# Attention output turned by DMA for 31 of 32 pairs of heads, in place of 16, and another written order of the attention's steps

## The chip, the cores and the metric

The kernel runs on one core of one Trainium2 chip. The metric is the device time of one execution in microseconds (us), lower is better. The engines are TensorE (PE in the profile; PEld is its weight load), VectorE (DVE), ScalarE (ACT), GpSimd (POOL) and SyncE (SP, which here only issues DMAs). Each engine runs its own instructions strictly in the order in which they were written into the program.

## The reference

Two stages, cut to what matters:

```python
def phi(x):
    proj = np.einsum('bhsd,df->bhsf', x, w_phi)
    proj = proj - np.max(np.abs(proj), axis=-1, keepdims=True)
    return np.concatenate([np.exp(proj), np.exp(-proj)], axis=-1)
q_p, k_p = phi(q), phi(k)                  # q, k, v: 8 batches, 8 heads, 576 tokens, 64
kv = einsum('bhsf,bhsd->bhfd', k_p, v);  z = k_p.sum(axis=2)
x = (q_p @ kv) / (q_p @ z + 1e-6)          # -> 4608 tokens x 512

P = exp(x @ w_gate - max)                  # 8 experts
for _ in range(8):                         # Sinkhorn routing
    P /= P.sum(1); P /= P.sum(0); P *= N / E
out = sum_e P[:, e] * (relu(x @ w1[e]) @ w2[e])     # w1: 512x1024, w2: 1024x512
```

## The kernel before

**Attention.** The unit of work is a pair of heads of one batch: 8 batches of 4 pairs, 32 in all. A pair's 576 tokens are 512 "main" tokens in four tiles of 128, and 64 "rest" tokens that all four pairs of a batch share as one extra tile. For a pair, TensorE projects k and q (L622), DVE takes the maxima (`maxes`, L614), ACT the exponentials (`exp`, L618), POOL scales v, TensorE forms kv and then the numerators with the denominator as a 65th column (L905), and DVE scales them, takes the reciprocal (L918) and writes the quotient to the tile `xb` (L919), tokens on the partitions.

**Turning.** The expert stage needs x with features on the partitions, in the resident tile `xT`. `pair_c` does this for the 512 main tokens of one pair, in one of two ways. On TensorE: four 128x128 transposes against an identity into a PSUM bank (L934), then one DVE copy of 128x512 to `xT` (L937). By DMA: one transposing DMA of 128 KB on SP's queue (L928), which reads `xb` and writes `xT`, with no PSUM bank and no DVE work. Before the change batches 3 to 6, 16 pairs, go by DMA and the rest by TensorE. The rest tokens of a batch always go by TensorE (`rest_c`, L944, copies L949). `gate` (16 tiny matmuls per 512 tokens) and expert 0's first product then read `xT`.

**Expert 0 as fill.** Expert 0 needs no routing weights, so its matmuls are put among the attention's: `up0` (8 matmuls of 512 columns over `xT` and w1, then ReLUs on ACT into `hx`, L983) and `down0` (8 matmuls of 512 columns over `hx` and w2). 24 such ups and 20 downs are written among the attention's steps; 12 ups and 16 downs more follow it and cover the routing, a chain of small DVE operations with one tiny matmul (L1179, output of `cs`) in each of 8 iterations. Then come experts 1 to 7 (L1466, L1475), the bulk of the time.

**What sets the order.** Each operation is recorded with a cost, its reads and writes, and its buffers. `Plan.schedule` then runs a model of the engines and of the two DMA queues: at each point the operation that can start first goes next, ties to the one recorded earlier, and the result is the written order of every engine. The string `order` sets in which order the attention's steps are recorded, one letter a step: `l` and `e` load q, k, v and the rest tokens; `w` loads a piece of expert 0's weights; `t` turns raw q and k by DMA (L567); `r` is the rest tokens' part; `a`, `q`, `p` are k's part, q's maxima and q's features of the next pair; `b` forms kv, `n` and `m` the outputs of the pair's two heads; `c` is `pair_c`; `g` is `rest_c` and `gate` of a batch; `u` and `d` are one `up0` and one `down0`.

SP's queue carries the loads of q and k for batches 0 and 1 (L544), of v (L558) and of rest tokens (L600, L607), the turning of raw q and k (L567, L686), and the turned outputs (L928). POOL's queue carries the casting loads of q and k for the other batches (L550, L605) and of expert 0's weights (L527, L531), between POOL's own arithmetic.

Of the kernel before, what the change touches and what calls it, by code (L numbers as in the profile page):

```python
# [349 lines left out]
def kernel(  # L350
# [13 lines left out]
    B, H, S, D = q.shape  # L364
# [4 lines left out]
    NP = H // 2  # L369
# [43 lines left out]
    def pe(cols, fn, r=(), w=(), takes=()):  # L413
        plan.op("PE", max(cols / 2400.0 + 0.0025, 0.031), 0.22, fn, r, w, takes)
# [4 lines left out]
    def dve(el, fn, r=(), w=(), shared=False):  # L419
        plan.op("DVE", el / 960.0 + 0.07, 0.15, fn, r, w, shared=shared)  # L420
# [7 lines left out]
    def dma(queue, nbytes, rate, fn, r=(), w=()):  # L428

        speed, unit = LINK.get(rate, (rate, 40))  # L430
        if nbytes == 2 << 20:
            speed, unit = 400, 150
        o = plan.op(queue, 0.8 if queue == "POOL" else 0.6, 0.0, fn, r, w, (), nbytes / speed)
        o.turn, o.unit = rate == 148, unit
# [71 lines left out]
    def new(tag):  # L506
        return R[tag].new()

    def bf(buf):

        return buf().bitcast(BF16)
# [412 lines left out]
        return xb, outs  # L924

    def pair_c(b, pr, xb):
        if b in (3, 4, 5, 6,):
            dma("SP", 1 << 17, 148, lambda: nc.sync.dma_start_transpose(  # L928
                out=xT[:, pr, b * SM:(b + 1) * SM].rearrange("p (a c) -> p a c", c=128),
                in_=xb()[:, 0:NJ].rearrange("p a b -> p (a b)")), [(xb, 0), (xb, 1)], [("xT", b, pr)])  # L930
            return
        pxt = new("PP")
        for j in range(NJ):
            pe(128, lambda j=j: nc.tensor.transpose(  # L934
                bf(pxt)[:, j * 128:j * 128 + 128], xb()[:, j, :], ident),
                [(xb, 0), (xb, 1), "ident"], [pxt])
        dve(270, lambda: nc.vector.tensor_copy(  # L937
            out=xT[:, pr, b * SM:(b + 1) * SM], in_=bf(pxt)[:, 0:512]),
            [pxt], [("xT", b, pr)])
# [150 lines left out]
    def stage_g(b):  # L1090
# [7 lines left out]
             "r": stage_r, "b": stage_b,  # L1098
             "n": lambda j: kvs[j](0), "m": lambda j: kvs[j](1),
             "c": lambda j: pair_c(j // 4, j % 4, xbs[j]), "g": stage_g,  # L1100
             "u": lambda i: up0(i // 4, i % 4), "d": lambda i: down0(i // 4, i % 4)}
    order = (
        "lraeaepqbwlqaqawwabwmqlltnrbppnwqbppmrmanbqaqmwwacmpnpbccpwbtcnmqnaqbclupunm"
        "taumquglcapalbcpnqqdcenmucugbblnapmrcqdutabnqpmunpbambccddnqplanmqmducpblttb"
        "augnaqlnrbdcampcadmqeutunqcppmdcaqtdqabpbbmlrqtdnpmuaqualbnagnacctbmqulupran"
        "tdpmtdqcmdnpdabdancpcabbqmpumqbcdgnappqunburqcbugmmnqdcdanumupqbnucmcpnmbddp"
        "bqmpncncubncmmgccg"
    )
    for i, n in enumerate(order):
        at[0] = i  # L1110
# [948 lines left out]
```

## Time and profile before

| | |
|---|---|
| median of 3 runs | 1009.96 us (1009.75 to 1012.1) |
| span of the profiled execution, first to last instruction | 1008.8 us |
| attention and its fill, by the last L905 and L937 | 0 to about 203 us |
| transposing DMAs of the output (L928) | 16 |
| TensorE transposes of the output (L934) and their DVE copies (L937) | 64 and 16 |
| granted TensorE clock | 1.000 |

The profile is one execution. Of the medians' 1009.96 us, 1008.8 us lie between its first and last instruction. Busy time of PE is modelled: matmuls are pipelined, each shown with its full latency, so the price of a matmul in a row of them is read from the distance between starts, not from its duration.

### The profile page before, as it was taken

What the parts mean: (1) busy time and instruction counts of PE and PEld (TensorE: products, weight loads), DVE (VectorE), ACT (ScalarE), POOL (GpSimd) and SP (SyncE); (2) the same over time, 40 slices, a digit from 0 to 9 for tenths busy, and PEclk for the clock granted to TensorE, in tenths of its full rate; (3) what the DMA queues carried; (4) which work ended last, traced back from release to release, by engine and by line L of the source; (5) the groups of instructions that cost most, each with busy time, mean ns of one, the idle gap of its engine ahead of it and who ended that gap; (6) DMA issues with size and microseconds to landing.
All of it is one profiled execution on the core that took longest, in us unless ns stands there. A gap on an engine that the chain in (4) does not pass through costs nothing.

```text
span 1008.8 us, 23309 instructions
## 1 busy us (share of the span) xinstructions
PE 994.0 (99%) x8376; PEld 727.7 (72%) x8376; DVE 898.6 (89%) x1999; ACT 812.8 (81%) x1930; POOL 447.6 (44%) x514
## 2 busy tenths in 40 slices
PE   7899999999999999999999999999999999999998
PEld 5666666644566877777777877787778777787775
DVE  7999998987888998899989898989889988989886
ACT  7999999845979788878878788777887888778874
POOL 5778674400133344434444444444443444344443
PEclk9999999999999999999999999999999999999999
DMA  9999999181136423282327133632246222724653
GB/s 249 183 202 183 157 153 144 38 170 56 53 121 143 147 97 98 84 184 96 109 98 170 44 100 131 130 127 98 97 117 177 97 98 84 147 79 142 208 174 126
DMA packets 129748, 128.86 MB, mean 128 GB/s; under 512 B 55776, under 2 KB 98272, under 8 KB 129632
## 3 DMA queue, kind: packets, MB, share of 16 engines
q1 hardware_dynamic: 97680, 103.33, 36.3%
q0 software_dynamic: 31648, 23.86, 16.9%
q8 instruction: 65, 1.06, 0.5%
q14 instruction: 51, 0.42, 0.2%
q10 hardware_dynamic: 304, 0.20, 0.1%
HBM read 122.50 MB, written 19.53 MB: 141 GB/s over the span
## 4 chain that ended last, share of the span: by engine, by line
PE 92%; DVE 3%; ACT 2%; DMA 2%; issue 1%; POOL 0%; DVEq 0%
PE ps L1466 41%; PE ps L1475 20%; PE ps L622 17%; PE ps L1607 11%; PE ps L905 2%; DMA xi6t<-X 1%; DMA xi<-X 1%; PE ps L752 1%; ACT q L618 0%; DVE m L614 0%; ACT k L618 0%; DVE wx L614 0%; DVE X L1240 0%; DMA acc<-in_k_dram 0%; DVE hs L1676 0%
## 5 line engine op out<-in xcount | busy, mean ns | idle before, releaser
L1875 POOL TENSOR_TENSOR acc<-acc,hx 128x512 f32<-128x512 f32 x186 | 236.1, 1276 | 404.7 <-ACT hx L1872 135.0
L1466 PEld LDWEIGHTS <-hs 128*128 128x128 bf16 x1984 | 194.1, 98 | 46.4 <-issue 0.2
L1872 ACT ACTIVATE hx<-ps,P 128x256 f32<-128x256 f32 x372 | 158.9, 483 | 53.4 <-PE ps L1466 52.0
L1860 DVE SCALAR_TENSOR_TENSOR acc<-ps,P,acc 128x256 f32<-128x256 f32 x372 | 162.2, 478 | 30.2 <-PE ps L1466 28.2
L1475 PE MATMUL ps<-xT,T 128*128 128x512 bf16 x608 | 171.0, 379 | 0.0
L1466 PEld LDWEIGHTS <-hx 128*128 128x128 bf16 x1488 | 145.6, 98 | 24.9
L1466 PE MATMUL ps<-hx,hs 128*128 128x256 bf16 x992 | 144.3, 273 | 0.0
L1676 DVE CUSTOM_DVE_ANT_0 hs<-ps,U 128x512 bf16<-128x512 f32 x192 | 124.7, 684 | 11.3 <-PE ps L1475 6.6
L1607 PE MATMUL ps<-xT 128*128 128x256 bf16 x576 | 125.4, 272 | 0.0
L1475 PEld LDWEIGHTS <-T 128*128 128x128 bf16 x672 | 65.8, 98 | 40.6
L1682 ACT ACTIVATE hs<-ps 128x512 bf16<-128x512 f32 x96 | 55.9, 598 | 41.7 <-PE ps L1475 40.2
L1466 PE MATMUL ps<-wx,hs 128*128 128x256 bf16 x560 | 78.4, 273 | 0.0
L622 PE MATMUL ps<-w,hx 128*128 128x512 bf16 x288 | 73.0, 379 | 0.0
L622 PE MATMUL ps<-xT,w 128*128 128x512 bf16 x288 | 72.9, 379 | 0.0
L1466 PE MATMUL ps<-wx,hx 128*128 128x256 bf16 x496 | 72.3, 273 | 0.0
L1676 DVE CUSTOM_DVE_ANT_0 hs<-ps,X 128x512 bf16<-128x512 f32 x96 | 65.1, 684 | 7.8 <-PE ps L1607 6.9
L1466 PE MATMUL ps<-hx 128*128 128x256 bf16 x496 | 71.2, 273 | 0.0
L1607 PEld LDWEIGHTS <-xT 128*128 128x128 bf16 x576 | 56.3, 98 | 17.5
L1466 PE MATMUL ps<-w,hx 128*128 128x256 bf16 x432 | 62.2, 273 | 0.0
L614 DVE TENSOR_REDUCE m<-ps 128x4 f32<-128x512 f32 x88 | 58.8, 680 | 3.7 <-PE ps L622 1.9
L1672 ACT COPY X<-ps 128x512 f32<-128x512 f32 x96 | 58.6, 610 | 2.5 <-DVE ps L1650 2.5
L1466 PE MATMUL ps<-w,hs 128*128 128x256 bf16 x432 | 60.2, 273 | 0.0
(174 smaller groups left out, 2256.0 us busy)
## 6 DMA issues: line engine op xcount, KB each, us to landing
xT<-xi SPq DMA_DIRECT2D x48, 448.0 KB, 4.6
xT<-xd SPq DMA_DIRECT2D x72, 256.0 KB, 4.0
wx<-in_moe_w_dram POOLq DMA_DIRECT2D x8, 1024.0 KB, 11.2
v_m<-in_v_dram SPq DMA_DIRECT2D x15, 512.0 KB, 5.2
out_dram<-acc SPq DMA_DIRECT2D x14, 512.0 KB, 3.0
w<-in_moe_w_dram POOLq DMA_DIRECT2D x6, 1024.0 KB, 11.0
xT<-xp SPq DMA_DIRECT2D x24, 256.0 KB, 2.8
qk<-in_k_dram POOLq DMA_DIRECT2D x12, 256.0 KB, 5.4
```

The source lines that it names most:

```text
L614: dve(el, lambda: nc.vector.tensor_reduce(out=dst(), in_=src(), axis=AX.X, op=ALU.max, apply_absolute_value=True), r, w)
L622: nc.tensor.matmul(out_, lhsT=lhsT, rhs=rhs, start=start, stop=stop)
L905: pe(65, lambda j=j: nc.tensor.matmul(pn()[:, j * D1:j * D1 + D1], lhsT=s["T"][x]()[:, j % 2, 2 * h + j // 2, :] if j < 4 else r["T"][x]() ...
L1466: pe(256, lambda i=i, k=k, z=z: nc.tensor.matmul(bank()[:, 256 * i:256 * i + 256], lhsT=lhs(k, i), rhs=rhs(k), start=first and z, stop=k = ...
L1475: pe(512, lambda k=k: nc.tensor.matmul(bank().rearrange("p (a b) -> p a b", a=2), lhsT=lhs(k), rhs=rhs(k), start=first and k == 0, stop=k ...
L1607: pe(256, lambda: nc.tensor.matmul(halves_of(bank[q], n)(), lhsT=lhs(), rhs=t()[:, rhs, :], start=start, stop=True, skip_group_check=True) ...
L1672: act(512, lambda: nc.scalar.copy(out=flat(to[q])(), in_=bank[q]()), [bank[q]], [(to[q], 0), (to[q], 1)])
L1676: dve(515, lambda: nc.vector._custom_dve(ADD_SAT, out=out_(q, i, j), in0=bank[q]().rearrange("p (a b) -> p a b", a=2), in1=to[q](), s0=3.0 ...
L1682: act(512, lambda: nc.scalar.activation(out=out_(q, i, j), in_=bank[q]().rearrange("p (a b) -> p a b", a=2), func=ACT.Relu, bias=0.0, scal ...
L1860: dve(320, lambda n=n, ts=ts: nc.vector.scalar_tensor_tensor(out=acc[g][:, ts, 256 * j:256 * j + 256], in0=bank()[:, 256 * n:256 * n + 256 ...
L1872: act(370, lambda n=n: nc.scalar.activation(out=u()[:, n, :], in_=bank()[:, 256 * n:256 * n + 256], func=ACT.Copy, bias=0.0, scale=P[:, 4 ...
L1875: pool(695, lambda: nc.gpsimd.tensor_tensor(out=acc[g][:, 2 * i:2 * i + 2, 256 * j:256 * j + 256], in0=acc[g][:, 2 * i:2 * i + 2, 256 * j: ...
```

## The change

`pair_c` sends every pair but the very last, (batch 7, pair 3), by DMA. That is 15 pairs more: batches 0, 1 and 2, and three pairs of batch 7. The string `order` is another one, with the same count of each letter.

```diff
     def pair_c(b, pr, xb):
-        if b in (3, 4, 5, 6,):
+        if (b, pr) != (B - 1, NP - 1):
             dma("SP", 1 << 17, 148, lambda: nc.sync.dma_start_transpose(
                 out=xT[:, pr, b * SM:(b + 1) * SM].rearrange("p (a c) -> p a c", c=128),
...
     order = (
-        "lraeaepqbwlqaqawwabwmqlltnrbppnwqbppmrmanbqaqmwwacmpnpbccpwbtcnmqnaqbclupunm"
...
+        "raqllbaapqenwalqabrpnmwwpwbmmnwwqqbpmbcwtpnecacapqqwacgllupbmpqlanqnubcnttbl"
...
```

Since the planner makes the order anew, rows move on every engine in the attention's part. From the expert stage on the orders agree: the last 70 per cent of the rows stand in the same order on PE, ACT, DVE and SP.

SP's queue early in the attention, before (`v_m` and `v_r` are v, `qk` and `qk_r` raw q and k, `qkT` and `rT` the same turned; a number behind x counts equal rows):

```order
L544 DMA acc_79<-in_q_dram 128x4x256
L607 DMA v_r<-in_v_dram 64x8x64 x2
L686 DMA_TRANSPOSE rT<-qk_r 128x4x128 x2
L558 DMA v_m<-in_v_dram 128x4x256
L567 DMA_TRANSPOSE qkT<-qk 128x16x128 x2
L558 DMA v_m<-in_v_dram 128x4x256 x2
L567 DMA_TRANSPOSE qkT<-qk 128x16x128
```

The same place of SP's queue now:

```order
L607 DMA v_r<-in_v_dram 64x4x64
L928 DMA_TRANSPOSE xT<-xb 128x4x128 x2
L558 DMA v_m<-in_v_dram 128x4x256
L607 DMA v_r<-in_v_dram 64x8x64 x2
L567 DMA_TRANSPOSE qkT<-qk 128x16x128
L928 DMA_TRANSPOSE xT<-xb 128x4x128 x2
L558 DMA v_m<-in_v_dram 128x4x256
L928 DMA_TRANSPOSE xT<-xb 128x4x128
L686 DMA_TRANSPOSE rT<-qk_r 128x4x128 x2
L928 DMA_TRANSPOSE xT<-wx 128x4x128
```

The outputs of batch 0 now stand in this queue, pairs 0 and 1 ahead of a load of v, pairs 2 and 3 behind the first turning of raw q and k; before, the queue held no L928 here.

DVE around the last outputs of batch 0, before (L937 is the copy of a turned pair; the last `xb` of batch 0 is the row `xb<-ps,wx`, whose reciprocal lies in the tile wx):

```order
L919 TENSOR_TENSOR xb<-ps,rec 128x5x64
L937 COPY xT<-ps 128x512
L913 TENSOR_TENSOR ps<-ps,r 128x325
L937 COPY xT<-ps 128x512 x2
L918 RECIPROCAL wx<-ps 128x5
L919 TENSOR_TENSOR xb<-ps,wx 128x5x64
L614 TENSOR_REDUCE m<-ps 128x4
L614 TENSOR_REDUCE m_r<-ps 128x2x2 x2
L892 COPY kv<-ps 128x260
L937 COPY xT<-ps 128x512
```

The same place on DVE now:

```order
L919 TENSOR_TENSOR xb<-ps,wx 128x5x64
L614 TENSOR_REDUCE wx<-ps 128x4
L614 TENSOR_REDUCE m<-ps 128x4
L614 TENSOR_REDUCE wx<-ps 128x4
L892 COPY kv<-ps 128x260
L614 TENSOR_REDUCE m<-ps 128x4
L614 TENSOR_REDUCE wx<-ps 128x4
L614 TENSOR_REDUCE m<-ps 128x4
L614 TENSOR_REDUCE wx<-ps 128x4
L614 TENSOR_REDUCE m<-ps 128x4
L949 COPY xT<-ps 64x4x64 x2
```

The four copies L937 of batch 0 are gone; behind the last `xb` stand eight maxima of later pairs, and then the copies of batch 0's rest tokens, which now come before the first fill instead of well after it.

More of the change, by code (lines that the diff above doesn't have):

```diff
@@ L1102 @@
     order = (
-        "lraeaepqbwlqaqawwabwmqlltnrbppnwqbppmrmanbqaqmwwacmpnpbccpwbtcnmqnaqbclupunm"
[L1104 to L1107, printed above, removed]
+        "raqllbaapqenwalqabrpnmwwpwbmmnwwqqbpmbcwtpnecacapqqwacgllupbmpqlanqnubcnttbl"
+        "munuaadrcptqmtcmculabmapabdqmrnaqpuneucbqdnmupaqacbdpmctlnbcdqumaplblntmgpuq"
+        "dabanlntpdqqacupqbrmguebccndnqmaaltbcpdalrumbqnpdqbcgmqpuubabcmnmpqundctqrcp"
+        "nbdagmpatuadnmubpmauaqnnbdpbncmuqdpqccncbmpmtccddgnpauqbprqbdpbanmmdmdnucnmu"
+        "cpqpbccqnumbgnmccg"
     )
```

## The prediction, on record before the changed kernel ran

> **What bounds the kernel now.** I read the page first, its busy shares and its chain of waits.
>
> ```profile
> PE 994.0 (99%) x8376; PEld 727.7 (72%) x8376; DVE 898.6 (89%) x1999; ACT 812.8 (81%) x1930; POOL 447.6 (44%) x514
> ...
> PE 92%; DVE 3%; ACT 2%; DMA 2%; issue 1%; POOL 0%; DVEq 0%
> ```
>
> PE is shown busy nearly always and carries 92% of the chain. Since its busy time is modelled, I asked the waits of PE, first from 60 us to the end, then for the first 60 us (the four longest).
>
> ```profile
> PE ps L1475 <- DVE hs L1530: 0.6, 1, 0.6
> PE ps L622 <- DVE cs L1179: 0.4, 1, 0.4
> ```
>
> ```profile
> PE ps L752 <- DMA acc<-in_k_dram: 4.0, 1, 4.0
> PE ps L622 <- DVE wx L614: 0.7, 3, 0.3
> PE ps L622 <- ACT k L618: 0.6, 1, 0.6
> PE ps L622 <- DVE m L614: 0.6, 2, 0.3
> ```
>
> The reader is to see that from 60 us on PE waits for others 1.0 us in all, and that ahead of 60 us it waits for the first load and then, in many small pieces, for DVE and ACT. The busy times by stretch say the same:
>
> ```profile
> core 0: us, PE busy (x) PEld busy (x) DVE busy (x) ACT busy (x) POOL busy (x), PEclk, DMA share, GB/s
> 0.00:50.00 50.00, 40.64 (x413) 28.06 (x413) 44.11 (x93) 44.31 (x111) 32.37 (x61) 1.00 1.19 216
> 50.00:200.00 150.00, 149.63 (x1788) 99.08 (x1786) 138.81 (x325) 143.76 (x352) 99.91 (x158) 1.00 0.96 148
> ```
>
> So there are two regimes. Up to about 50 us DVE and ACT set the pace and PE lacks work; from then on PE is full, and the kernel's end is the sum of PE's work plus what PE idled before. A us of PE work removed anywhere is a us of time, as long as ACT (143.76 of 150 us busy in the attention) keeps up.
>
> **The change part by part.** *Removed from PE: 15 pairs x 4 transposes.* Their price is the distance between starts, not the 0.38 us of a row:
>
> ```profile
> 45.48 0.38 PE L622 MATMUL ps<-xT,w 128*128 128x512 bf16 x1
> ...
> 49.14 0.60 PE L622 MATMUL ps<-wphi,qkT 128*128 128x256 bf16 x4
> 49.57 0.29 PE L905 MATMUL ps<-wx 128*128 128x65 bf16 x4
> ...
> 50.10 0.38 PE L934 MATMUL ps<-ident,xb 128*128 128x128 bf16 x4
> 50.32 1.03 PE L622 MATMUL ps<-xT,w 128*128 128x512 bf16 x4
> 51.18 0.28 PE L905 MATMUL ps<-wx 128*128 128x65 bf16 x4
> ```
>
> Four transposes take 50.10 to 50.32, 0.22 us, 0.055 each. 60 x 0.055 = 3.3 us less PE work. All of it counts: the transposes before the fill begins only enter the next term instead.
>
> [...]
>
> *Removed from DVE: 15 copies L937.* Two in a row took 41.92 to 42.67, some 0.33 us from start to start:
>
> ```profile
> 37.14 2.48 DVE L614 TENSOR_REDUCE wx<-ps 128x4 f32<-128x512 f32 x4
> ...
> 41.92 0.75 DVE L937 COPY xT<-ps 128x512 bf16<-128x512 bf16 x2
> 42.81 0.49 DVE L919 TENSOR_TENSOR xb<-ps,wx 128x320 bf16<-128x320 f32 x1
> ...
> 45.42 0.43 DVE L937 COPY xT<-ps 128x512 bf16<-128x512 bf16 x1
> ```
>
> That is 15 x 0.33 = 5.0 us less on DVE. After 50 us PE covers it and it is worth nothing by itself; it gives DVE the room to follow a faster PE. Ahead of 50 us, where DVE is a bound, only batch 0's four copies matter, and they are part of the next term.
>
> *Moved: the beginning.* In the new order 25 fewer matmuls stand on PE ahead of the first fill matmul (324, against 349): 8 of 256 columns, 5 of 512, and 12 of 128. By the rows above a 256 costs 0.43 / 4 = 0.108 and a 512 costs 0.86 / 4 = 0.215, so 0.86 + 1.08 + 0.66 = 2.6 us. ACT, too, has less ahead of its first ReLU of the fill (L983): four exponentials of 512, four of 256 and three small ones.
>
> ```profile
> 28.07 1.26 ACT L618 ACTIVATE kr<-ps 128x256 bf16<-128x256 f32 x4
> 29.12 1.19 ACT L618 ACTIVATE qr<-ps 128x512 bf16<-128x512 f32 x2
> 30.07 0.32 ACT L618 ACTIVATE r_r<-m_r 128x4 f32<-128x4 f32 x1
> 30.17 0.71 ACT L618 ACTIVATE q<-ps 128x512 bf16<-128x512 f32 x1
> ...
> 33.30 2.16 ACT L618 ACTIVATE q<-ps 128x512 bf16<-128x512 f32 x4
> 35.21 0.35 ACT L618 ACTIVATE em<-m 128x16 f32<-128x16 f32 x1
> ...
> 48.34 0.78 ACT L983 ACTIVATE hx<-ps 128x512 bf16<-128x512 f32 x1
> ```
>
> From start to start a 512 is 1.91 / 4 = 0.48, a 256 is 1.05 / 4 = 0.26, a small one 0.10: 1.9 + 1.05 + 0.3 = 3.3 us. ACT is packed there, so the fill begins about 3.3 us earlier (42 us instead of 45.5), with 2.6 us less PE work ahead: PE idles 3.3 - 2.6 = 0.7 us less before it. Bounds: at best, the idle of the first 50 us, 50 - 40.64 less the first 4.0, 5.4 us, goes altogether; at worst the fill waits for its data.
>
> *The wait that this brings.* PE's queue holds the first fill and gate 0 where xT of batch 0 must have landed, and everything of the attention behind them. What is late next if it has not: kv and outputs of batch 1 (L905), then DVE and ACT. The turning DMAs that exist now:
>
> ```profile
> L928 SPq DMA_TRANSPOSE xT<-xb x10: 1189/1195/1723, 94.5 to 188.4; - x10
> ...
> DMA to landing us min/median/max: 2.3/4.6/7.2
> ```
>
> The cover is on DVE: between the last `xb` of batch 0 and the rest tokens' copies stand eight maxima and a kv copy, and four maxima took 2.48 us: 2 x 2.48 + 0.4 = 5.4 us. A median landing of 4.6 us is hidden; the slowest, 7.2, would cost 1.8; the slowest of the raw turnings in that busy time, 10.3 below, 4.9. Without cover a median would cost 4.6. I take 0.2, near the median.
>
> *Added to the DMA engines and SP.* One transposing DMA alone in a quiet stretch, from 188 to 192 us:
>
> ```profile
> 188.00:192.00 4.00, 4.00 (x36) 2.23 (x33) 3.80 (x10) 4.00 (x10) 1.72 (x2) 1.00 0.15 33
> ```
>
> 0.15 x 4 = 0.6 us of all 16 engines; 15 of them are 9 us, 12 in the first 100 us, where the share is over 1. Loads come up to 7 us later in the sum of that stretch, and 15 x 1.2 us more issue on SP. That costs nothing while nobody waits for loads: after the first load no wait for a load stands among PE's waits above. Uncovered it is the slow rival below.
>
> *The end of the attention.* The last pair stays on PE, so the gate of batch 7 waits at most for pair 2's landing, 2.3 to 4.6 us against some 3 us of DVE and PE work behind its last `xb`: 0 to 1.6 us, I take 0.1. The rows after that are the same as before, and cost the same.
>
> *Sum.* -3.3 - 0.7 + 0.2 + 0.1 = -3.7 us. The profiled span of 1008.8 becomes 1005.1; the runs lie 1009.96 - 1008.8 = 1.2 us above it, which stays: 1006.3 us. Since the bounds of the beginning reach further down (-5.4) than the median landing reaches up, I put it at 1006.0.
>
> **The rivals.** *ACT takes over: no change.* ACT is busy 143.76 of 150 us. If its 6.2 idle us are its own, PE cannot pull ahead, and PE idles the 3.7 us that it gained: 1010 us. For it: ACT's work is the same in both orders, 96% busy. Against it: most of that idle is made by PE itself.
>
> ```profile
> ACT hx L983 <- PE ps L622: 4.5, 9, 1.1
> ACT k L618 <- PE ps L622: 0.9, 1, 0.9
> ACT wx L618 <- PE ps L622: 0.8, 1, 0.8
> ```
>
> 4.5 + 0.9 + 0.8 = 6.2 us of waiting for PE can shrink with it, so a gain of 3.7 fits, but barely. [...]
>
> *SP's queue blocks: slower.* Pairs 2 and 3 of batch 0 now stand in SP's queue behind a raw turning (L567) that waits for loads from POOL's queue, and later outputs stand ahead of loads of v.
>
> ```profile
> SPq L567 <- DMA qk<-in_q_dram: 28.6, 6, 10.2
> SPq L928 <- DVE m L614: 28.0, 9, 7.2
> ...
> ```
>
> ```profile
> DMA to landing us min/median/max: 4.3/5.8/10.3
> ```
>
> One wait of 10.2 us there delays xT of batch 0 by as much: 10.2 + 4.6 - 5.4 = 9.4 us of PE, in place of the 0.2, so -3.7 + 9.2 = +5.5: 1015.5 us. It decides for slower, by more than 3.0 us, from a wait of about 7.5 us on. Against it: no engine waits for a raw turning now, so the loads are early at present.
>
> *More from the beginning.* The fill, which begins earlier and has fewer holes, takes the whole 5.4 us of early idle: -3.3 - 5.4 = -8.7, 1001.3 us. Against: DVE and ACT, both packed from 15 us on, still set when work arrives.
>
> **How the numbers follow.** 0.3% (3.0 us) is about what a measurement of this kernel can tell from no change. The forecast (1004.2 to 1008) has 0.56, with 0.08 of it above 1006.9, where it counts as the same; ACT 0.21; the blocked queue and its smaller kin 0.12; more from the beginning 0.11. Faster: 0.48 + 0.11 = 0.59; same: 0.08 + 0.21 = 0.29; slower 0.12. The range leaves out the slow case and the extreme of the fast one: 1003.0 to 1011.5; the forecast's own is 1004.2 to 1008.
>
> **What would show it.** Right: the waits of PE after 60 us stay near 1 us, the first L622 with xT starts near 42 us, L934 has 4 rows, and the first matmul of expert 1 (L1475) comes about 4 us earlier. ACT's rival shows as waits of PE for ACT between 60 and 200 us, the blocked queue as a wait of PE for the DMA xT<-xb around 40 us, or of POOL for v_m. The prediction is wrong if attention ends no earlier although PE has less to do, or if rows after 310 us cost another time than before.

## The result, and the profile after

The change made the kernel slower: 1040.0 us (median of 4 runs, 1038.6 to 1041.2) against 1009.9 us (4 runs, 1009.5 to 1012.1), a ratio of 1.0293, 95% interval 1.0280 to 1.0306. The forecast was 1006.0 us, faster. The profiled execution spans 1039.2 us, 30.4 more than the one before.

The page of the changed kernel, its busy times and its chain of waits:

```profile
PE 997.8 (96%) x8316; PEld 726.5 (70%) x8316; DVE 895.8 (86%) x1984; ACT 813.7 (78%) x1930; POOL 447.9 (43%) x514
...
PE 86%; DMA 8%; DVE 3%; ACT 1%; issue 1%; POOL 0%; SPq 0%; DVEq 0%; POOLq 0%; ACTq 0%
```

PE has 60 matmuls less, as the change says, and yet its share fell from 99% to 96%. In the chain DMA went from 2% to 8%: work now waits for transfers. Where, the first matmuls of expert 1 tell (L1475, in the timeline of PE; columns are start, length, operation). Before the change, and after it:

```profile
244.31 0.81 PE L1475 MATMUL ps<-xT,wx 128*128 128x512 bf16 x3
```

```profile
274.92 0.59 PE L1475 MATMUL ps<-xT,wx 128*128 128x512 bf16 x2
```

That stage begins 30.6 us later, and from there to the end both kernels take the same time: 1008.8 - 244.3 = 764.5 and 1039.2 - 274.9 = 764.3. So the whole loss lies in the attention with its fill. The waits of PE in the first 275 us of the changed kernel (total, times, longest):

```profile
PE ps L622 <- DMA xT<-xb: 8.7, 4, 3.8
PE ps L622 <- DMA xT<-wx: 8.5, 3, 7.4
PE ps L622 <- DMA rT<-qk_r: 5.7, 1, 5.7
PE ps L752 <- DMA acc<-in_k_dram: 3.6, 1, 3.6
PE ps L622 <- DMA qkT<-qk: 2.4, 2, 1.4
```

The fourth row is the first load, as before (4.0). The others are new, and each is a matmul that stands for a transposing DMA: for turned outputs (`xT`) 8.7 + 8.5 = 17.2 us, for turned raw q and k (`rT`, `qkT`) 8.1 us, 25.3 us together in ten waits. In the kernel before there is no such row.

The waits cost more than their length. Busy times by stretch around the longest one (PE busy, PEld, DVE, ACT, POOL, then the granted clock, DMA share, GB/s):

```profile
79.00:80.00 1.00, 0.00 (x0) 0.00 (x0) 0.34 (x1) 0.00 (x0) 0.00 (x0) 0.92 2.27 160
80.00:81.00 1.00, 0.00 (x0) 0.00 (x0) 0.00 (x0) 0.00 (x0) 0.36 (x1) 0.50 2.69 91
...
84.00:85.00 1.00, 0.10 (x1) 0.09 (x1) 0.00 (x0) 0.00 (x0) 0.00 (x0) 0.50 1.12 278
...
89.00:90.00 1.00, 1.00 (x5) 0.58 (x4) 0.95 (x2) 0.21 (x2) 0.70 (x1) 0.50 1.28 290
90.00:91.00 1.00, 1.00 (x22) 0.81 (x20) 0.00 (x0) 0.88 (x2) 1.00 (x1) 0.96 0.35 75
```

Two things are to be seen. While PE stands, DVE and ACT run dry as well, since what would feed them is queued on PE behind the waiting matmul. And PE begins again at a granted clock of 0.50 in place of 1.00, from 84.9 until 90 us. There five matmuls of 512 columns in a row (L622) go from 84.91 to 86.99 us, 0.42 us from start to start; at 1.00 five go from 93.30 to 94.38, 0.22 us. So 5 us at half speed are 2.5 us more (an estimate).

Together the two account for the loss. Up to the start of expert 1, before the change and after it, and then the four stretches in which the changed kernel's clock was 0.50 (same columns):

```profile
0.00:244.31 244.31, 234.22 (x2447) 147.76 (x2448) 220.61 (x524) 206.09 (x492) 134.02 (x220) 1.00 0.92 154
```

```profile
0.00:274.92 274.92, 238.43 (x2389) 146.86 (x2390) 217.76 (x509) 206.64 (x492) 133.88 (x220) 0.95 0.87 144
```

```profile
45.71:52.53 6.82, 4.89 (x31) 2.45 (x32) 1.79 (x3) 2.84 (x7) 0.00 (x0) 0.50 1.16 129
79.84:90.08 10.24, 5.17 (x20) 2.46 (x20) 1.85 (x4) 2.58 (x7) 3.04 (x7) 0.50 1.42 191
110.56:113.97 3.41, 3.34 (x25) 1.73 (x25) 0.98 (x3) 1.09 (x2) 3.34 (x6) 0.50 1.37 191
172.00:178.83 6.83, 3.38 (x26) 2.29 (x27) 2.31 (x4) 1.47 (x5) 0.73 (x3) 0.50 0.99 144
```

PE idles 274.92 - 238.43 = 36.5 us in place of 10.1, 26.4 more. In the four stretches it works for 16.8 us; at the full clock, by the 0.42 and 0.22 us above, half of that would do, so about 8.4 us are the clock's (an estimate). Without them its work is 230.0 us, 4.2 less than before: 26.4 + 8.4 - 4.2 = 30.6 us.

### The profile page after: what moved, and what is told of

Its sections match the earlier page's. It is cut to its first block, busy times and chain, and to the rows that moved or that the text cites. A ratio compares the mean times of both kernels' runs of the same rounds, so it can differ in the third digit from the quotient of the medians.

```text
span 1039.2 us, 23200 instructions
## 1 busy us (share of the span) xinstructions
PE 997.8 (96%) x8316; PEld 726.5 (70%) x8316; DVE 895.8 (86%) x1984; ACT 813.7 (78%) x1930; POOL 447.9 (43%) x514
## 4 chain that ended last, share of the span: by engine, by line
PE 86%; DMA 8%; DVE 3%; ACT 1%; issue 1%; POOL 0%; SPq 0%; DVEq 0%; POOLq 0%; ACTq 0%
PE ps L1466 40%; PE ps L1475 19%; PE ps L622 14%; PE ps L1607 11%; DMA xT<-wx 2%; DMA xT<-xb 2%; PE ps L905 1%; DMA qkT<-qk 1%; DMA xp<-xT 1%; DMA rT<-qk_r 1%; DMA xi6t<-X 1%; DMA xi<-X 1%; PE ps L752 1%; DVE m L614 0%; DVE X L1240 0%
## 5 line engine op out<-in xcount | busy, mean ns | idle before, releaser
L1475 PE MATMUL ps<-xT,T 128*128 128x512 bf16 x608 | 171.1, 379 | 0.0
L1475 PEld LDWEIGHTS <-T 128*128 128x128 bf16 x672 | 65.7, 98 | 40.6 <-issue 0.2
L622 PE MATMUL ps<-xT,w 128*128 128x512 bf16 x288 | 78.6, 395 | 10.6 <-DMA xT<-wx 8.5
L1682 ACT ACTIVATE hs<-ps 128x512 bf16<-128x512 f32 x96 | 55.9, 598 | 41.8 <-PE ps L1475 40.5
L622 PE MATMUL ps<-w,hx 128*128 128x512 bf16 x288 | 73.2, 379 | 0.2 <-DVE m L614 0.2
L983 ACT ACTIVATE hx<-ps 128x512 bf16<-128x512 f32 x72 | 43.3, 627 | 27.6 <-PE ps L622 27.1
## 6 DMA issues: line engine op xcount, KB each, us to landing
wx<-in_moe_w_dram POOLq DMA_DIRECT2D x8, 1024.0 KB, 11.1
```

The lines of the kernel that those rows point to most:

```text
L622: nc.tensor.matmul(out_, lhsT=lhsT, rhs=rhs, start=start, stop=stop)
L983: act(512 * n, lambda f0=f0, ph=ph, ht=ht: nc.scalar.activation(out=ht()[:, f0 % 4:f0 % 4 + n, :].rearrange("p a b -> p (a b)"), in_=ph()[ ...
L1475: pe(512, lambda k=k: nc.tensor.matmul(bank().rearrange("p (a b) -> p a b", a=2), lhsT=lhs(k), rhs=rhs(k), start=first and k == 0, stop=k ...
L1682: act(512, lambda: nc.scalar.activation(out=out_(q, i, j), in_=bank[q]().rearrange("p (a b) -> p a b", a=2), func=ACT.Relu, bias=0.0, scal ...
```

## The experiments

Three theories stood at the start. **A**: the written order counts on transposing DMAs that land later than it assumes, and the engine that needs them stands with everything behind it. **B**: the new order is bad by itself, whatever lands. **C**: 15 more DMAs load the DMA engines. After the second group A was split: **A2** is A, and POOL's queue stands in the same way.

### First group: the two halves of the change, and more room in the plan

The old `order` with the new condition (edits here are shown against the changed kernel):

```diff
-        "raqllbaapqenwalqabrpnmww...
+        "lraeaepqbwlqaqawwabwmqll...
```

> 31 pairs by DMA as in the change, but the order of steps of before; the planner places the rows anew. Late landing (theory A: PE stands at matmuls that need a DMA-turned output, which lands later than the plan expects, 24.5 us of waits and a lowered clock behind them): batches 0 to 2 are turned by DMA here too, so waits of PE for DMA xT of 5 to 25 us, 1015 to 1035 us. The order alone (theory B): no loss, about 1006 us. DMA load (theory C: 15 more transposes slow every load, whoever waits): about 1035 us, with waits for loads and not for xT.

The new `order` with the old condition:

```diff
-        if (b, pr) != (B - 1, NP - 1):
+        if b in (3, 4, 5, 6,):
```

> The new order of steps with 16 pairs by DMA as before. Theory A: no batch whose output is needed at once is turned by DMA except 3 to 6, so few waits for xT, 1006 to 1018 us. Theory B: 1035 us or more. Theory C: about 1010 us.

The changed kernel with the four pairs of batch 0 back on TensorE:

```diff
-        if (b, pr) != (B - 1, NP - 1):
+        if b and (b, pr) != (B - 1, NP - 1):
```

> The change with batch 0 alone back on TensorE (27 pairs by DMA). Theory A: the two waits at 43 and 47 us, 6.1 us, go with the lowered clock behind them, the later ones (7.4, 2.1, 5.7) stay: 1027 to 1033 us. Theory B and C: within 3 us of 1040.

The planner told that a turning DMA lands 5 us later than it assumed (so it writes the reading matmul later):

```diff
-                o.end = landed[0] + 1.0
+                o.end = landed[0] + (6.0 if o.turn else 1.0)
```

> The change, with the planner told that every transposing DMA lands 5 us later; the same operations, written in another order that leaves them more room. Theory A: most of the 24.5 us of waits for DMA go, 1006 to 1020 us. Theory B: the recorded order of steps is the same, so 1030 us or more. Theory C: the same DMAs run, 1030 us or more.

| kernel | median, us | ratio to before, 95% interval |
|---|---|---|
| old order, 31 by DMA (e1) | 1029.2 | 1.0200 (1.0179 to 1.0221) |
| new order, 16 by DMA (e2) | 1025.1 | 1.0147 (1.0126 to 1.0169) |
| new order, batch 0 on TensorE (e3) | 1029.4 | 1.0183 (1.0167 to 1.0200) |
| new order, plan with 5 us more (e4) | 1035.8 | 1.0254 (1.0239 to 1.0269) |

Neither half is good alone: the order, with the plan that follows from it, costs half of the loss with no DMA added. Batch 0 by DMA costs 1040.0 - 1029.4 = 10.6 us in this order, as A said. The others don't fit a single theory: e1 lies in A's range, but PE's waits for `xT` that A named did not come; e2 lies in no theory's range; e4 lies where B and C put it. The new order with the old condition shows these waits of PE, and of POOL (in a run of 1028.2 us, the slowest of four):

```profile
PE ps L622 <- DMA rT<-qk_r: 3.9, 1, 3.9
PE ps L622 <- DMA qkT<-qk: 3.8, 2, 2.0
```

```profile
POOL qk L550 <- DMA qkT<-qk: 11.0, 3, 3.8
```

So the order itself brings PE's waits for the raw turnings, and POOL stands too (below). Plan e4 removed most of PE's waits for DMAs:

```profile
PE ps L622 <- DMA xT<-xb: 3.6, 1, 3.6
PE ps L622 <- DVE m L614: 2.8, 6, 0.9
PE ps L622 <- DMA rT<-qk_r: 1.6, 1, 1.6
```

and gained only 4 us. This looked like B. But with another plan nearly everything moves. In e4 expert 1 (the first L1475) begins at 261.3 us, 13.6 earlier than in the changed kernel, and the stage from there to the end takes 1034.2 - 261.3 = 772.9 us in place of 764.3; in e1 it takes 1026.0 - 257.05, about 769. So most of what e4 won in the attention was lost again behind it; why that stage got longer was not found. Changing the plan is therefore no clean test, and the following experiments leave the plan and the written order as they are.

### Second group: the same order, but PE reads nothing that a DMA turned

A constant block of `xT`, filled once at the start and overwritten only by the last pair, stands in for what the DMAs deliver. All DMAs are still issued, in the same places.

```diff
+    flat = xT[:, NP - 1, (B - 1) * SM:B * SM]
+    nc.vector.memset(flat, 0.01)
...
-                    xT[:, dc, (4 * g + ti) * 128:(4 * g + ti + 1) * 128], wgate[:, dc, :],
+                    flat[:, 128 * ti:128 * ti + 128] if g < 7 else
+                    xT[:, dc, (4 * g + ti) * 128:(4 * g + ti + 1) * 128], wgate[:, dc, :],
...
-                        xT[:, dc, g * 512:(g + 1) * 512], dc == 0, dc == NP - 1),
+                        flat if w and g < 7 else xT[:, dc, g * 512:(g + 1) * 512],
+                        dc == 0, dc == NP - 1),
```

> The changed kernel with the same written order and the same 31 DMAs, but the matmuls of the fill and of the gate for groups 0 to 6 read a constant block of xT (filled once at the start) in place of the turned attention outputs; so PE no longer waits where a turned output lands late. Left out: routing and the first expert's products are of constants, the output is not the reference's. The raw halves turned by DMA (qkT, rT) are still read and waited for. Theory A (late landings of turned outputs): PE's waits for xT are 16.3 us in the changed kernel's trace and part of its lower clock follows them; 1015 to 1024 us. Theory B (the new order alone is slow, whatever lands): 1035 to 1041. Theory C (31 more DMAs load the DMA engines so that the other loads come late): 1030 to 1040, with PE's waits moved to qkT, rT and weights.

The next three add or use the same for the raw halves, in `rest_a` and `pair_a`:

```diff
-        tokens(pp, lambda c: rT()[:, c, :], NP, [rT], own)
+        tokens(pp, lambda c: rT()[:, c, :] if b < 2 else flat[:, 128 * c:128 * c + 128], NP,
+               [rT], own)
...
             o = 2 * h0 + c
+            if b >= 2:
+                return flat[:, 128 * c:128 * (c + n)]
```

On the changed kernel, with the edit above:

> As the last, and besides the feature matmuls of batches 2 to 7 read the constant block in place of the raw q and k turned by DMA (qkT, rT). The DMAs are all still issued, in the same order; PE waits for none of their results while attention runs. Left out: attention of batches 2 to 7 is of constants, the output is not the reference's. Theory A extended to every DMA that turns: about 1003 to 1010, the written order being as good as the old one when nothing that a transposing DMA delivers is waited for. Theory B: 1020 to 1041. Theory C: the DMA engines are as loaded as in the changed kernel, 1020 or more, with PE waiting for loads that are not turned (v, weights).

Both edits on the kernel before, as a control:

> Control: the edit of the last run made to the kernel before. Left out: attention of batches 2 to 7 and the first expert's products are of constants. Theory A: the old order hardly waits for turning DMAs, so 1004 to 1011. If the edit itself makes the kernel much faster (under 1000), the last run's gain says nothing of waits.

The edit of the raw halves alone, on e2 (new order, old condition):

> The new written order with the old condition (outputs of batches 3 to 6 turned by DMA, the others by TensorE), and the feature matmuls of batches 2 to 7 read the constant block in place of qkT and rT. Left out: attention of batches 2 to 7 is of constants. The same without the constants took 1025.1 us. Theory A extended to the raw halves: PE waited 2.0, 1.8 and 3.9 us for qkT and rT there, so 1005 to 1014. Theory B: 1022 to 1027.

| kernel | median, us | ratio to before, 95% interval |
|---|---|---|
| changed, fill and gates read no turned output (e5) | 1024.2 | 1.0157 (1.0124 to 1.0190) |
| and features read no turned q and k (e6) | 1016.4 | 1.0063 (1.0039 to 1.0087) |
| control: both edits on the kernel before (e7) | 1010.0 | 0.9999 (0.9990 to 1.0008) |
| e2, features read no turned q and k (e9) | 1021.5 | 1.0113 (1.0098 to 1.0128) |

The control says that the edit by itself gains nothing. In the changed kernel it gave back 15.8 us and then 7.8 us, with order, instructions and DMAs unchanged. That is A, against B and C. But e5 lies just past the upper end of what A expected (1024), and e6 and e9 miss A's numbers by 6 us or more: something was left. In e6, between 20 and 200 us:

```profile
POOL qk L552 <- DMA qkT<-qk: 8.0, 2, 4.6
...
PE ps L624 <- POOL v L821: 3.8, 1, 3.8
PE ps L910 <- ACT qr L620: 3.2, 1, 3.2
```

POOL issues the casting loads of raw q and k (L550 of the changed kernel, L552 here). There are two buffers, and the load of the next half has to wait until the turning DMA has read the old one. POOL stands at that load, and its products for v are queued behind it; PE waits for those, and the other wait has the same root. The changed kernel's POOL has the row too, the kernel before has none:

```profile
POOL qk L550 <- DMA qkT<-qk: 7.5, 3, 3.0
```

### Third group: a third place for raw q and k

Every third half is loaded into part of `acc` 4, which is idle then. The planner still counts two buffers, so the order stays.

```diff
     ring(a_in, [128, 2, 4, NJ * D], BF16, "qk", 2)
+    def third(i):
+        made[0] += 1
+        n = made[0]
+        if n % 3 == 2 and n < 9:
+            return acc[4].rearrange("p a b -> p (a b)").bitcast(BF16)[:, 0:2048].rearrange(
+                "p (a b c) -> p a b c", a=2, b=4)
...
+    R["qk"].make = third
```

On e6, on the changed kernel as it is, and on e2:

> The kernel of e6_no_dma_turned (PE reads no result of a turning DMA; 1016.4 us), and every third raw half of q and k of batches 2 to 6 is loaded into a place of its own (part of acc 4, idle then) in place of the two buffers in turn. The plan and the written order stay. Left out: as there. In e6's trace POOL stood 8.0 us, twice, at the load of the next raw half until the turning DMA had read the buffer, with the products by L821 behind it, for which PE then waited 3.8 us, and ACT's qr in the same way 3.2 us. Theory A2 (the late raw turnings also stop POOL's queue, and PE behind it): 1007 to 1012. Theory B (the rest is the new order itself): 1014 to 1019.

> The changed kernel, complete, with the third place for raw halves alone; the plan and the written order stay. POOL's waits for qkT<-qk are 7.5 us there in three pieces. Theory A2: they go, but most of the 16.3 us in which PE waits for turned outputs and the 5.7 for rT stay; 1028 to 1037. If PE's waits alone count (theory A without POOL): 1037 to 1041.

> The new written order with the old condition (1025.1 us), complete, and the third place for raw halves. POOL's waits there are 11.0 us in three pieces, and PE and ACT have few others. Theory A2: 1011 to 1018. Theory B: 1022 to 1027.

e10 came to 1012.3 us, 1.0021 (1.0000 to 1.0041), and its chain of waits showed one such wait left, where the edit ended (`n < 9`):

```profile
139.12 9.51 DMA qkT<-qk
...
149.19 0.81 POOL qk L563
150.03 1.92 POOL wx L826
152.32 1.89 PE ps L635 x18
```

Here a raw turning took 9.5 us, then POOL issued the load, then formed a product, and then PE went on. The ten runs of e10 spread from 1006.1 to 1018.3 us, those of the control from 1009.5 to 1010.9; the fastest of e10 had a mean clock of 1.000, and its time is that of the next kernel. The last experiment of the group drops `and n < 9`:

> The kernel of e10_no_turned_third_qk with the third place for raw halves used to the end (halves of batches 6 and 7 too). Left out: as in e6. In e10's trace one wait was left: POOL stood 4.9 us until qkT<-qk had read a buffer, PE then 4.3 us for a product of POOL's at 152 us, and the granted clock of that stretch of 25 us was 0.86. Theory A2, with the gain that was predicted for a kernel that waits for no turning DMA (-3.7 us): 1003 to 1009, and no wait of PE over 2 us between 25 and 240 us. If the removed transposes are worth nothing, or the added DMAs cost PE in another way: 1010 to 1013 without such a wait.

It took 1006.5 us, 0.9958 (0.9941 to 0.9974). Its longest waits of PE in the first 275 us, and the start of expert 1:

```profile
PE ps L766 <- DMA acc<-in_k_dram: 3.9, 1, 3.9
PE ps L635 <- DVE wx L627: 1.5, 3, 1.1
```

```profile
240.48 0.81 PE L1493 MATMUL ps<-xT,wx 128*128 128x512 bf16 x3
```

No wait but the first load is long, and expert 1 begins 244.3 - 240.5 = 3.8 us earlier than before the change. The new order, the 31 DMAs and the removed transposes are all in this kernel: neither the order (B) nor the load on the DMA engines (C) costs anything by itself. Nor do the transposing DMAs land earlier here. From issue to landing (minimum, median, maximum in us) the 31 outputs, and then the raw halves of q and k, take

```profile
DMA to landing us min/median/max: 2.3/5.5/9.5
```

```profile
DMA to landing us min/median/max: 5.9/8.4/9.9
```

against medians of 3.8 and 6.3 in the changed kernel. What costs is standing for results and buffers of transposing DMAs. (The third place was not tried on the kernel before; POOL has no wait for a raw turning there that it could take away.)

The other two were smaller than expected. e12 came to 1022.5 us, 1.0113 (1.0092 to 1.0134), 2.6 less than e2 where 7 and more were expected: POOL's wait fell from 11.0 to 2.4 us, but PE's own waits for raw turnings rose from 7.7 to 9.1. e11 came to 1038.9, 1.0287 (1.0269 to 1.0305), no different from the changed kernel: POOL's row is gone, but the longest wait for `xT` grew from 7.4 to 10.1 us. In e11's waits of PE (total, times, longest):

```profile
PE ps L633 <- DMA xT<-wx: 10.7, 2, 10.1
```

So the effects don't add: here, freeing one queue only moved the wait to another place. In the changed kernel the time returns only with all of them gone. For e2 no run took both kinds away at once, so most of the 14.8 us that it loses is not traced.

### Fourth group: a complete kernel that keeps the gain

Can a plan that knows of later landings keep the 1006.5 us with the right output? Here the planner adds 1.2 us to each turning DMA, and the steps are put in a new order for it (`order` is other letters, with the same count of each), with 27 pairs by DMA, with 20, and each with the third place (`n < 9`).

```diff
-                o.end = landed[0] + 1.0
+                o.end = landed[0] + (2.2 if o.turn else 1.0)
...
-        if (b, pr) != (B - 1, NP - 1):
+        if b > 0 and (b, pr) != (B - 1, NP - 1):
```

For 20 pairs the condition is `b in (2, 3, 4, 5, 6)`.

> Complete. 27 pairs by DMA (batches 1 to 6 and three pairs of batch 7), the planner told that a turning DMA lands 1.2 us later than it had assumed, and an order of steps chosen anew for that, starting from the changed kernel's. Theory A2: the new matmuls stand later behind their turning DMAs, so PE's waits for them shrink, but the order is derived from the tight one; 1006 to 1016. If 1.2 us of room is too little: 1015 to 1030.

> Complete. 20 pairs by DMA (batches 2 to 6), the same 1.2 us, and an order chosen anew starting from the order before. 4 pairs less for PE are 16 x 0.055 = 0.9 us; the rest would come from a fuller beginning. Theory A2: 1006 to 1012 if the waits stay away as in the kernel before; 1013 to 1025 if any order chosen by a plan is broken by late landings.

> e15_new_plan_27 and the third place for raw halves, complete. Theory A2: as that one or up to 4 us faster, since POOL does not stand for the raw turnings; if POOL's queue has nothing to do with it, the same.

> e16_new_plan_20 (1021.7 us) and the third place for raw halves, complete. In e16's trace a raw turning landed after 12.7 us, POOL stood 7.5 us for its buffer, and DVE's ps (L913) and PE's L905 stood 6.8 us behind it; POOL's three such waits are 12.4 us. Theory A2: 1009 to 1016. If POOL's waits for the raw turnings are not what PE pays for: 1019 to 1023.

| kernel | median, us | ratio to before, 95% interval |
|---|---|---|
| 27 by DMA, new plan (e15) | 1035.1 | 1.0240 (1.0224 to 1.0256) |
| the same, third place (e17) | 1032.0 | 1.0218 (1.0201 to 1.0236) |
| 20 by DMA, new plan (e16) | 1021.7 | 1.0110 (1.0095 to 1.0125) |
| the same, third place (e18) | 1017.6 | 1.0070 (1.0051 to 1.0089) |

None beats the kernel before. e15 lies 5 us beyond even its worse range, e16 within its worse one, and e18 between its two; e17 gained 3.1 us, as A2 said. The waits are the same kind. In e16 one chain ran from a raw turning of 12.7 us over POOL and DVE to PE:

```profile
99.30 12.67 DMA qkT<-qk
...
112.53 0.78 POOL qk L550
...
114.92 0.52 DVE ps L913
...
115.48 0.44 PE ps L905 x5
```

The third place took it away (e18, 4.1 us less; a gain of at least 5.7 had been expected), and the next was a wait of PE for `xT` of 3.9 us, 2.1 in e16. In complete kernels POOL's waits are thus paid too, once PE's own are few. The 1.2 us of room was not enough, 5 us (e4) made another plan that is slow in other places; an order between them that holds was not found.

## Why the prediction was wrong

**The gain was predicted rightly, and the chip has it.** The sum's -3.3 for the transposes and -0.7 for the beginning say -4.0; e14 differs from the kernel before by 1006.5 - 1010.4, some -4.0 us, and expert 1 begins 3.8 us earlier, where about 4 were forecast. Taken one by one the terms agree less well: PE's work at the full clock fell by 4.2 us by the working above (forecast 3.3), and in e10, which begins like e14, PE idles 9.2 us of the first 60 in place of 9.7 (forecast 0.7 less). That the sum agrees so closely is in part luck. In the changed kernel itself the first L622 with `xT` starts at 40.5 us (forecast near 42), and the rows after the attention cost the same, as forecast.

**The step that failed is "the wait that this brings": "I take 0.2, near the median".** It is wrong in size and in scope. In size: the two waits for `xT<-xb` in the first 60 us, at gate 0, come to 6.1 us, above even the stated bound of 4.9. The last quotient `xb` of batch 0 is written by 37.2 us, and the gate needs it soon after, turned:

```profile
36.69 0.48 DVE L919 TENSOR_TENSOR xb<-ps,wx 128x320 bf16<-128x320 f32 x1
```

```profile
41.19 0.20 PE L622 MATMUL ps<-wgate,xT 128*128 128x8 bf16 x2
43.66 0.18 PE L622 MATMUL ps<-wgate,xT 128*128 128x8 bf16 x1 [2.28 <-DMA xT<-xb]
47.64 0.51 PE L622 MATMUL ps<-wgate,xT 128*128 128x8 bf16 x13 [3.80 <-DMA xT<-xb]
```

The turning of pair 3 is issued at 38.8 us, behind that of pair 2, and lands at 47.6, 10.4 us after that quotient. PE came to it at 43.66 - 2.28 = 41.4 us. So the cover was 4.2 us and not 5.4: the prediction counted it up to the rest tokens' copies on DVE, which the gate of the first 512 tokens does not read. 10.4 - 4.2 = 6.2 us is the price. The landings that were set against the cover had been measured from 94 to 188 us, where fewer transfers were under way (DMA share 0.84 from 100 to 200 us before the change; 1.17 and then 1.64 from 40 to 50 us after it). The chain of waits of the changed kernel gives this landing 8.8 us, and up to 120 us four more behind it:

```profile
38.80 8.80 DMA xT<-xb
...
60.70 6.69 DMA xT<-wx
...
69.19 5.11 DMA qkT<-qk
...
75.64 9.22 DMA xT<-wx
...
103.52 7.07 DMA xT<-xb
```

At the first of them SP issued the turnings of pairs 2 and 3, and POOL at the same time five loads of expert 0's weights:

```profile
37.48 2.83 SPq L928 DMA_TRANSPOSE xT<-xb  x2
```

```profile
37.16 1.17 POOL L527 DMA_DIRECT2D w<-in_moe_w_dram  x2
38.31 1.45 POOL L531 DMA_DIRECT2D w<-in_moe_w_dram  x2
...
39.94 0.70 POOL L531 DMA_DIRECT2D w<-in_moe_w_dram  x1
```

Whether these loads delayed the turning was not tried by itself. In scope: the term priced batch 0 alone. The waits for outputs of later batches (17.2 - 6.1 = 11.1 us), for raw q and k (8.1 us) and on POOL had no term at all.

**"That costs nothing while nobody waits for loads" failed with it.** It took the absence of such waits in the trace of before as a property of the kernel. It was a property of the old order, which left room in front of each reader. The new order, by itself, spent that room: e2 waits 7.7 us for raw turnings on PE and 11.0 on POOL with no DMA added. The same holds for the argument against the blocked queue, "no engine waits for a raw turning now, so the loads are early at present".

**The rivals.** SP's blocked queue had the right sign, and its mark, a wait of PE for `xT<-xb` around 40 us, came. Its mechanism had a small part: the raw turning ahead of pairs 2 and 3 waited 1.8 us for its loads, not 10.2, and was being issued until 37.4 us; pair 2 followed at 37.5 and pair 3 at 38.8, 1.6 us after the last quotient. Both were issued by 40.3 us and landed late. Its price, +5.5 us, was for one place; there were ten. ACT as the new bound did not show: PE waits for it 1.2 us at most in one place after 60 us. More from the beginning did not come either.

**What had no place in the prediction** is the clock. It was 1.000 in the kernel before, and 0.987 after: PE's waits of 3.8, 7.4, 2.1 and 5.7 us for transposing DMAs were each followed by matmuls at 0.50, in the four stretches above; that is about 8.4 of the 30.6 us, by the estimate there.

**What stays open** is most of e1's loss. Its order is the old one, and PE's waits for DMAs are short (the longest but the first load 1.4 us). One more has the same root: at 94.8 us PE waits 2.5 us for a product of POOL's, which had stood 4.5 us at a load until a raw turning had read the buffer. Another 2.7 us is a wait in the routing. The rest is spread over stages that are all somewhat longer.

## What to carry to other kernels

- A trace without waits for a transfer says that the present order leaves it room, not that it has room in another order (e2, with no DMA added, waits 7.7 us on PE and 11.0 us on POOL where the kernel before does not wait). Where a change moves the readers, price each reader against the slowest landings of its own busy stretch, in every queue where it stands, also where a buffer must come free.
- A wait at the head of an in-order queue was paid here with what stood behind it (in e6 POOL stood 8.0 us at two loads, and PE 3.8 us for a product behind them); look for the queues (here POOL's) that issue transfers and also compute.
- To see whether waits are the cause, let the readers read something else that is ready, and keep order and transfers as they are; changing the plan instead moves everything.

## What the runs showed of the hardware

The landing times of equal transposing DMAs spread widely. From issue to landing, of the 31 outputs of 128 KB each (L928), and of the raw halves of 512 KB (L567), in the changed kernel, minimum, median and maximum in us:

```profile
DMA to landing us min/median/max: 2.3/3.8/9.2
```

```profile
DMA to landing us min/median/max: 4.6/6.3/11.1
```

The median of the outputs even fell, from 4.6 before, while the longest waits came from the few that took 7 to 9 us: here the slowest, not the median, set the price.

After a wait of 7.4 us PE's granted clock was 0.50 and stayed so for 5 us of full work. The four stretches at 0.50 last 6.8, 10.2, 3.4 and 6.8 us. Before the stretch from 110.56 us PE had waited 2.1 us; behind the wait of 3.6 us for the first load the clock stayed at 1.00. What sets it was not shown.
